# Scores one group ahead, and the mixer of one batch spread over the attention of the next

## The chip, the cores and the metric

The kernel runs on one core of a Trainium2 chip. The metric is the device time of one execution in microseconds (us). Not all kernels ran in the same rounds; before ran in all of them, and its median moved by 0.5 us between rounds. The profile is one further execution; its span is the time from the first to the last instruction, 1 to 4 us shorter than the timed runs.

## The reference, cut to what matters

Eight batches, each with a sequence of 3136 rows, 256 columns of u and v, 64 columns of z.

```python
def _attn_ref(u, v, z):                       # u, v: (8, 3136, 256); z: (8, 3136, 64)
    scores = np.matmul(z, z.transpose(0, 2, 1)) / S
    attn = np.maximum(scores, 0.0) ** 2
    return u * np.matmul(attn, v)

def _moe_ref(x, U, V, w_ch1, w_ch2):          # U: (3136, 32), V: (32, 3136), w: 256 to 1024 to 256
    h = x.transpose(0, 2, 1) @ U @ V
    u = x + h.transpose(0, 2, 1)
    ch = np.maximum(u @ w_ch1, 0.0) @ w_ch2
    return u + ch
```

The mixer of a batch needs `x.T @ U`, a sum over the whole sequence. It cannot begin before that batch's attention has ended. Different batches have nothing to do with each other.

## The kernel before

The sequence is padded to 25 tiles of 128 rows and handled in six groups of 512 columns and one narrow group of 128. For each group 13 pairs of score tiles are made (a pair fills one two-bank PSUM buffer, `ps2`, of which there are three), rectified, squared, and then multiplied with v into a one-bank buffer (`ps1`, two of them). "L169" in a profile line is line 169 of the kernel; the comments give these lines.

```python
for gi, (g0, gw) in enumerate(igroups):
    attn_sb = attn_pool.tile([P, NT, IGW], BF16, name="attn_sb")      # 2 buffers
    for jp in range(0, NT, 2):
        ps_s = ps2_pool.tile([P, 2, IGW], FP32, name="ps2")
        ...matmul(out=ps_s[:, jj, :gw], lhsT=zzT[...], rhs=zzT[:, g0 : g0 + gw])   # L169
        if (jp // 2) % 4 == 3:
            nc.vector.tensor_single_scalar(... op=ALU.max)            # L177, VectorE's share
        else:
            nc.scalar.activation(... func=AF.Relu)                    # L184, ScalarE's share
        nc.vector.tensor_tensor(... op=ALU.mult)                      # L189, the square
    for q0 in range(0, gtiles, 2):
        ...matmul(out=ps_o[:, qq, :], lhsT=attn_sb[...], rhs=v_bf[:, jt, :])       # L202
        ...x_bf = ps_o * u_sb                                         # L214, VectorE
# after the last group: t1 = U.T @ x (L223), copied on ScalarE (L231)
```

The mixer makes u2 transposed for all seven chunks first (L246 and L253, copied on ScalarE, L260). Then per chunk:

```python
for (c0, cw) in igroups:
    relu1_sb = relu1_pool.tile([P, NH, IGW], BF16, name="relu1_sb")   # 2 buffers
    for hp in range(0, NH, 2):
        ...16 matmuls in all, ps_m1 = w1.T @ u2T_bf                   # L270
        nc.scalar.activation(out=relu1_sb[...], in_=ps_m1, func=AF.Relu)           # L277
    for q0 in range(0, ctiles, 2):
        ...ps_f = t1 @ V + relu1 @ w2                                 # L289, L297
        ...out_sb = ps_f + x_bf, and the store                        # L305
```

The loop over the batches, with the weights loaded and cast ahead of it:

```python
emit_prep(0)          # z: load, cast, 25 transposes; v: 7 loads and casts (L150), all casts on ScalarE
for b in range(B):
    emit_attention(b)
    if b + 1 < B:
        emit_prep(b + 1)
    emit_mixer(b)
```

The order of these statements is not quite the order on an engine, since the framework that builds the kernel has a scheduler. In the trace of before, scores of the next group stand among the attention-times-v matmuls of this one, although the code has one block after the other.

## Time and profile before

| | before |
|---|---|
| time, median of 13 runs | 1374.5 us |
| span of the profile | 1372.8 us |
| TensorE matmuls laid end to end ("dense", worked out in the prediction) | 1262.7 us |
| start of the first batch's U matmuls | 134.6 us |
| steady period, from one batch's U to the next one's | 167.9 us |

The prediction shows the lines that carry its reading. One further line of the groups of before gives busy us and mean ns of one instruction, then the engine's idle time ahead of these instructions and what ended it:

```profile
L184 ACT ACTIVATE attn_sb<-ps 128x1024 bf16<-128x1024 f32 (+3 forms) x560 | 457.8, 912 | 390.1 <-PE ps L169 364.0
```

### The profile page before, as it was taken

How to read it: one execution, taken by the hardware profiler on the slowest of the kernel's cores; microseconds unless marked ns; L12 is line 12 of the kernel's file. 1: busy time of each engine (PE TensorE's matmuls, PEld its weight loads, DVE VectorE, ACT ScalarE, POOL GpSimd, SP SyncE). 2: the span in 40 equal slices, each digit the busy share in tenths (PEclk: the TensorE clock that was granted, in tenths of full speed). 3: DMA queues.
4: the chain of work that ended last, by engine and by line, in shares of the span. 5: the costliest groups of instructions: out<-in, count | busy, mean ns of one | idle time of the engine just before them, and what ended most of it. 6: DMA issues, size and time to landing. Idle time of an engine off the chain costs nothing.

```text
span 1372.8 us, 23038 instructions
## 1 busy us (share of the span) xinstructions
PE 1326.4 (97%) x10008; PEld 913.3 (67%) x10008; DVE 707.9 (52%) x1104; ACT 793.0 (58%) x976; POOL 23.7 (2%) x41
## 2 busy tenths in 40 slices
PE   3999999999999999999999999999999999999998
PEld 1677666676666766667666676666766667666665
DVE  1776147751477414774167732677217772177721
ACT  6854855557555575556655565655655555455554
POOL 2000000000000000000000000000000000000000
PEclk9999999999999999999999999999999999999999
DMA  9611421124111241111511115111131111111101
GB/s 236 183 32 31 145 70 32 32 64 134 49 32 32 65 148 41 32 32 57 148 49 32 32 49 159 38 32 32 57 102 33 32 32 34 62 34 32 32 32 65
DMA packets 109542, 87.89 MB, mean 64 GB/s; under 512 B 32832, under 2 KB 109120, under 8 KB 109440
## 3 DMA queue, kind: packets, MB, share of 16 engines
q1 hardware_dynamic: 109440, 86.41, 21.0%
q8 instruction: 78, 1.28, 0.4%
q14 instruction: 24, 0.20, 0.0%
HBM read 60.70 MB, written 25.69 MB: 63 GB/s over the span
## 4 chain that ended last, share of the span: by engine, by line
PE 75%; ACT 21%; DMA 2%; issue 1%; DVE 1%; ACTq 0%; SPq 0%; POOL 0%
PE ps L202 40%; PE ps L169 19%; ACT relu_sb L277 12%; PE ps L297 10%; ACT attn_sb L184 4%; PE ps L270 4%; ACT u2T_bf L260 3%; ACT zzT L135 2%; PE ps L223 2%; DMA v_raw<-in_v_dram 1%; PE ps L289 1%; ACT v_bf L150 0%; DMA wtmp<-in_moe_w_ch_dram 0%; DVE attn_sb L189 0%; DVE out_sb L305 0%
## 5 line engine op out<-in xcount | busy, mean ns | idle before, releaser
L184 ACT ACTIVATE attn_sb<-ps 128x1024 bf16<-128x1024 f32 (+3 forms) x560 | 457.8, 912 | 390.1 <-PE ps L169 364.0
L202 PE MATMUL ps<-v_bf,attn_sb 128*128 128x256 bf16 x5000 | 619.8, 273 | 1.2
L202 PEld LDWEIGHTS <-attn_sb 128*128 128x128 bf16 x5000 | 466.9, 98 | 164.3 <-DVE attn_sb L189 62.0
L189 DVE TENSOR_TENSOR attn_sb<-attn_sb 128x1024 bf16<-128x1024 bf16 (+3 forms) x728 | 407.0, 608 | 73.6 <-ACT attn_sb L184 71.3
L169 PE MATMUL ps<-zzT 128*128 128x512 bf16 (+1 forms) x1400 | 340.6, 357 | 9.8 <-ACT attn_sb L184 6.4
L305 DVE TENSOR_TENSOR out_sb<-ps,x_bf 128x512 f32<-128x512 f32 (+1 forms) x104 | 69.7, 671 | 405.6 <-PE ps L297 404.0
L277 ACT ACTIVATE relu_sb<-ps 128x1024 bf16<-128x1024 f32 (+1 forms) x224 | 190.9, 937 | 141.4 <-PE ps L270 141.4
L297 PE MATMUL ps<-w_bf,relu_sb 128*128 128x256 bf16 x1600 | 209.6, 273 | 7.9 <-ACT relu_sb L277 7.3
L169 PEld LDWEIGHTS <-zzT 128*128 128x128 bf16 x1400 | 133.4, 98 | 107.1 <-issue 29.3
L177 DVE TENSOR_SCALAR attn_sb<-ps 128x1024 bf16<-128x1024 f32 (+1 forms) x168 | 185.1, 1102 | 6.1 <-PE ps L169 6.1
L270 PE MATMUL ps<-u2T_bf,w_bf 128*128 128x512 bf16 (+1 forms) x896 | 183.9, 356 | 3.9 <-ACT u2T_bf L260 2.6
L297 PEld LDWEIGHTS <-relu_sb 128*128 128x128 bf16 x1600 | 148.6, 98 | 50.5 <-ACT relu_sb L277 24.5
L214 DVE TENSOR_TENSOR x_bf<-ps,u_sb 128x512 bf16<-128x512 f32 (+1 forms) x104 | 69.8, 671 | 176.8 <-PE ps L202 168.2
L270 PEld LDWEIGHTS <-w_bf 128*128 128x128 bf16 x896 | 83.2, 98 | 87.4 <-issue 7.9
L150 ACT CAST v_bf<-v_raw 128x1024 bf16<-128x1024 f32 (+1 forms) x56 | 52.0, 965 | 23.5 <-DMA v_raw<-in_v_dram 14.9
L289 PE MATMUL ps<-t_sb,V_bf 128*128 128x256 bf16 x200 | 53.4, 273 | 0.0
L260 ACT CAST u2T_bf<-ps 128x1024 bf16<-128x1024 f32 (+1 forms) x56 | 48.1, 995 | 0.9 <-PE ps L253 0.9
L246 PE MATMUL ps<-ident,x_bf 128*128 128x128 bf16 x400 | 41.8, 219 | 0.3
L128 PE MATMUL ps<-ident,z_bf 128*128 128x128 bf16 x200 | 20.9, 228 | 19.9 <-ACT z_bf L121 19.3
L253 PE MATMUL ps<-V_bf,t_sb 128*128 128x512 bf16 (+1 forms) x112 | 38.3, 356 | 0.0
L246 PEld LDWEIGHTS <-x_bf 128*128 128x128 bf16 x400 | 30.3, 97 | 10.7 <-issue 4.5
L128 PEld LDWEIGHTS <-z_bf 128*128 128x128 bf16 x200 | 16.2, 102 | 25.9 <-issue 22.1
(25 smaller groups left out, 151.8 us busy)
## 6 DMA issues: line engine op xcount, KB each, us to landing
v_raw<-in_v_dram SPq DMA_DIRECT2D x48, 512.0 KB, 4.7
u_sb<-in_u_dram SPq DMA_DIRECT2D x96, 256.0 KB, 2.7
out_dram<-out_sb SPq DMA_DIRECT2D x96, 256.0 KB, 2.1
z_raw<-in_z_dram SPq DMA_DIRECT2D x8, 768.0 KB, 5.3
wtmp<-in_moe_w_ch_dram SPq DMA_DIRECT2D x4, 512.0 KB, 4.1
v_raw<-in_v_dram SPq DMA_DIRECT2D x8, 64.0 KB, 2.2
u_sb<-in_u_dram SPq DMA_DIRECT2D x8, 64.0 KB, 2.1
out_dram<-out_sb SPq DMA_DIRECT2D x8, 64.0 KB, 2.0
```

The lines of the kernel that those rows point to most:

```text
L169: nc.tensor.matmul(out=ps_s[:, jj, :gw], lhsT=zzT[:, (jp + jj) * P : (jp + jj + 1) * P], rhs=zzT[:, g0 : g0 + gw], start=True, stop=True,)
L177: nc.vector.tensor_single_scalar(out=attn_sb[:, jp : jp + npair, :gw], in_=ps_s[:, :npair, :gw], scalar=0.0, op=ALU.max,)
L184: nc.scalar.activation(out=attn_sb[:, jp : jp + npair, :gw], in_=ps_s[:, :npair, :gw], func=AF.Relu,)
L189: nc.vector.tensor_tensor(out=attn_sb[:, jp : jp + npair, :gw], in0=attn_sb[:, jp : jp + npair, :gw], in1=attn_sb[:, jp : jp + npair, :gw] ...
L202: nc.tensor.matmul(out=ps_o[:, qq, :], lhsT=attn_sb[:, jt, q * P : (q + 1) * P], rhs=v_bf[:, jt, :], start=(jt == 0), stop=(jt == NT - 1),)
L214: nc.vector.tensor_tensor(out=x_bf[:, it0 : it0 + nq, :], in0=ps_o[:, :nq, :], in1=u_sb[:, :nq, :], op=ALU.mult,)
L246: nc.tensor.matmul(out=ps_u2[:, db, q * P : (q + 1) * P], lhsT=x_bf[:, it, db * P : (db + 1) * P], rhs=ident, start=(q == 0), stop=False,)
L260: nc.scalar.copy(out=u2T_bf[:, :, c0 : c0 + cw], in_=ps_u2[:, :, :cw])
L270: nc.tensor.matmul(out=ps_m1[:, hh, :cw], lhsT=w1_bf[:, db, ht * P : (ht + 1) * P], rhs=u2T_bf[:, db, c0 : c0 + cw], start=(db == 0), stop ...
L277: nc.scalar.activation(out=relu1_sb[:, hp : hp + 2, :cw], in_=ps_m1[:, :, :cw], func=AF.Relu,)
L297: nc.tensor.matmul(out=ps_f[:, qq, :], lhsT=relu1_sb[:, ht, q * P : (q + 1) * P], rhs=w2_bf[:, ht, :], start=False, stop=(ht == NH - 1),)
L305: nc.vector.tensor_tensor(out=out_sb[:, :nq, :], in0=ps_f[:, :nq, :], in1=x_bf[:, it0 : it0 + nq, :], op=ALU.add,)
```

## The change

The intent: TensorE should never wait for something made a moment ago. There are four parts. (1) Scores run one group ahead of the attention-times-v that reads them. (2) The mixer of batch b-1 is spread over the attention of batch b, chunk k beside group k, with its final matmuls one group later. (3) The next batch is prepared in group 4 and its first group is scored in the last group of this one, so that batches overlap. (4) The weights are loaded after the first batch's z and v. No matmul, relu or square is added or removed. The functions are cut into pieces that a new main loop calls in 13 slots per group; the core of the diff, with cuts marked:

```diff
-    u2t_pool = ctx.enter_context(tc.tile_pool(name="u2t", bufs=1))     # one tile for all chunks
+    u2t_pool = ctx.enter_context(tc.tile_pool(name="u2t", bufs=2))     # one tile per chunk
...
-    for dd in range(ND):        # weight loads and casts
+    def emit_weight_loads():
...
     emit_prep(0)
-    for b in range(B):
-        emit_attention(b)
-        if b + 1 < B:
-            emit_prep(b + 1)
-        emit_mixer(b)
+    emit_weight_loads()
+    emit_score_pairs(0, 0, 0, NPAIR)
+    finals = iter(())
+    for b in range(B):
+        m = b - 1
+        for k in range(NG):
+            if k == NG - 3 and b + 1 < B:
+                emit_prep(b + 1)
+            nxt = (b, k + 1) if k + 1 < NG else (b + 1, 0)
+            atv = attn_v_steps(b, k)
+            n_atv = igroups[k][1] // P * NT
+            done = 0
+            for slot in range(NPAIR):                       # 13 slots
+                if nxt[0] < B:
+                    emit_score_pairs(*nxt, slot, slot + 1)
+                upto = (slot + 1) * n_atv // NPAIR
+                advance(atv, upto - done)
+                done = upto
+                if slot in (0, 1, 3, 4):
+                    advance(finals, 1)
+                if m >= 0:
+                    if slot == 2:
+                        emit_u2T(m, k)
+                    if slot in (5, 7, 9, 11):
+                        emit_m1(m, k, (slot - 5) // 2, (slot - 5) // 2 + 1)
+            advance(atv, 1000)
+            advance(finals, 1000)
+            if m >= 0:
+                finals = final_steps(m, k)
+        emit_attention_tail(b)                              # U matmuls and t1
+    ...the mixer of the last batch, alone: u2T one chunk ahead, finals one chunk behind
```

In the changed kernel the lines are: L172 scores, L187 and L180 relus, L192 square, L247 attention-times-v, L278 U, L153 cast of v, L124 to L138 z, L302 to L316 u2T, L330 first layer, L337 its relu, L411 and L419 finals.

## The prediction

> **What bounds the kernel now.** I read the page first: the span, the busy shares, the chain by engine and line.
>
> ```profile
> span 1372.8 us, 23038 instructions
> PE 1326.4 (97%) x10008; PEld 913.3 (67%) x10008; DVE 707.9 (52%) x1104; ACT 793.0 (58%) x976; POOL 23.7 (2%) x41
> ...
> PE 75%; ACT 21%; DMA 2%; issue 1%; DVE 1%; ACTq 0%; SPq 0%; POOL 0%
> ```
>
> TensorE is the only full engine, and 75% of the chain that ends last is its matmuls. But 97% says little: a matmul's end is modelled and successive ones overlap, so short waits do not show as idle. I therefore looked in the chain in order of time for blocks where TensorE runs one kind of matmul without a break, to get its true pace:
>
> ```profile
> 56.02 1.08 PE ps L169 x5
> 57.10 6.12 PE ps L202 x56
> 63.22 1.08 PE ps L169 x5
> ...
> 73.97 6.12 PE ps L202 x56
> ...
> 161.19 3.45 PE ps L270 x16
> ```
>
> A matmul of 512 columns (L169, L270) takes 3.45/16 = 0.216 us, one of 256 columns (L202) 6.12/56 = 0.1093 us, and there is no price for changing kind (57.10 + 6.12 = 63.22). The 128-column ones come at 0.055 us (four in 0.22 us at 141.5 us of TensorE's timeline).
>
> One batch has 150 score, 96 first-MLP and 12 V matmuls of 512 columns (258), 625 attention-times-v, 25 U and 225 final ones of 256 (875), and 118 of 128 (scores and MLP of the last narrow group, transposes). That is 1251, times 8 is 10008, as the page counts. Dense they need 258 x 0.216 + 875 x 0.1092 + 118 x 0.0555 = 55.7 + 95.6 + 6.5 = 157.8 us a batch, 1262.7 us for eight. So 1372.8 - 1262.7 = 110 us are lost, and the next question is where. The windows of one steady attention group and one steady mixer chunk:
>
> ```profile
> 73.97:90.83 16.86, 16.83 (x127) 11.86 (x126) 12.56 (x18) 9.03 (x11) 0.00 (x0) 1.00 0.13 33
> ```
>
> ```profile
> 176.41:184.21 7.80, 7.60 (x55) 4.92 (x53) 1.38 (x2) 3.77 (x4) 0.00 (x0) 1.00 0.19 67
> ```
>
> The attention group has 25 scores and 100 of the 256-column ones: 5.40 + 10.92 = 16.3 us dense, 16.86 taken, 0.56 lost. The chunk has 16 x 0.216 + 36 x 0.1092 = 7.4 dense, 7.80 taken, 0.4 lost. VectorE is busy 12.56 of 16.86 in the one and 1.38 of 7.80 in the other: the two stages load the helpers very unequally. The timeline shows what a wait looks like:
>
> ```profile
> 66.81 0.60 PE L202 MATMUL ps<-v_bf,attn_sb 128*128 128x256 bf16 x4
> 67.30 0.59 PE L169 MATMUL ps<-zzT 128*128 128x512 bf16 x2
> 67.73 0.60 PE L202 MATMUL ps<-v_bf,attn_sb 128*128 128x256 bf16 x4
> 68.22 0.59 PE L169 MATMUL ps<-zzT 128*128 128x512 bf16 x2
> ...
> 180.78 0.38 PE L297 MATMUL ps<-w_bf,relu_sb 128*128 128x256 bf16 x2
> 181.36 0.39 PE L297 MATMUL ps<-w_bf,relu_sb 128*128 128x256 bf16 x2 [0.20 <-ACT relu_sb L277]
> ```
>
> In the attention, four matmuls of a pair that has only just been squared take 0.49 us instead of 0.44, pair after pair: TensorE goes at the pace of VectorE (four pairs cost VectorE 4 x 0.62 + 1.2 = 3.7 us, TensorE 4 x 0.915 = 3.66 us). In the mixer TensorE waits for ScalarE's relu of the same chunk. Both are waits for something made a moment ago, and the list of waits agrees:
>
> ```profile
> PEld L202 <- DVE attn_sb L189: 62.0, 259, 0.6
> ...
> PEld L297 <- ACT relu_sb L277: 24.5, 67, 0.5
> ```
>
> Last the start, where the large piece is:
>
> ```profile
> 12.32 0.57 SPq L77 DMA_DIRECT2D z_raw<-in_z_dram  x1
> ...
> 17.66 1.53 ACT L121 ACTIVATE z_bf<-z_raw 128x1600 bf16<-128x1600 f32 x1
> ...
> 19.33 1.01 PE L128 MATMUL ps<-ident,z_bf 128*128 128x128 bf16 x8 [19.33 <-ACT z_bf L121]
> ```
>
> The last rows of z are asked for only at 12.3 us, behind weights and v, so TensorE does nothing for 19.3 us.
>
> The U matmuls end a batch's attention; they start at 134.57 us in batch 0 and at 1311.7 in batch 7. Sorting the 110 us by these: up to 134.57 us 103.4 dense, so 31.2 lost (3.4 of it in six groups, 27.8 the start proper); then seven periods of (1311.72 - 134.57)/7 = 168.2 against 157.8, 10.3 lost each, 72 in all; the rest 61.1 against 54.4, 6.7 lost. A period's 10.3 is 6 x 0.56 = 3.4 in groups, 6 x 0.4 = 2.5 in chunks, and about 4.4 where batch and stage change.
>
> **What the Trainium skill says.** "TensorE: Matmul & The Clock Gate", section "Wait — 56ns, not 53.3ns?", gives the start-to-start time of warm matmuls as columns / 2.4 GHz plus about 2.5 ns: 215.7 ns for 512, and by the same formula (an estimate) 109.2 for 256. The trace agrees: 215.6 and 109.3, with a new weight load before each. "Perfetto Trace Analysis", section "Identifying the Most-Contended Engine", says matmul busy time is a bad measure of headroom; here 97% busy goes with 8% lost. The same page, section "Optimization Strategy", proposes to interleave regimes whose limiting engine differs, which is this change; the two windows show regimes that differ. Its section "Matmuls" wants independent groups to rotate through PSUM banks so that evacuation overlaps; the three two-bank buffers (ps2) and two one-bank buffers (ps1) stay as they are.
>
> **The change, part by part.** No matmul, relu or square is added or removed; the dense 1262.7 us stays. What moves is the order in which work is offered.
>
> 1. Scores run one whole group ahead of attention-times-v. A matmul then reads a square made some 16 us earlier, so the 0.05 us per alternation goes. VectorE needs 12.6 us per group of 16.3, ScalarE 9.0: as averages both fit. I leave 0.1 us per group. Saved per period: 3.4 - 0.6 = 2.8.
>
> 2. The mixer of batch b-1 is spread over the attention of batch b, chunk k beside group k, its final matmuls one group later still. The mixed group has 16.3 + 7.4 + 0.9 (u2T) = 24.6 us of TensorE, against 12.6 + 1.4 = 14 us of VectorE and 9.0 + 3.8 + 1.0 = 13.8 us of ScalarE. The 2.5 us of chunk waits nearly goes; I leave 0.5. The two-bank buffers now serve scores, u2T and MLP in turn. In a slot with both a score pair and an MLP pair TensorE has 0.43 + 0.84 + 0.86 = 2.1 us, ScalarE at most 2 x 0.93 = 1.9: it fits, narrowly.
>
> 3. Batch changes. The 4.4 us fall to about 2: the next batch's first group is already scored when this one's attention ends, and u2T no longer runs as a stage of its own that ScalarE paces (about 1 us of copy per chunk against 0.86 us of matmuls). What remains: in the narrow last group TensorE has about 13 us and ScalarE and VectorE about 11.5 each, and the next batch's preparation puts 1.5 + 7 x 0.55 + 6.5 = 12 us on ScalarE in one group (about 26 us beside TensorE's 26), which the light narrow scores of the following group must absorb. So a period loses 0.6 + 0.5 + 2 = about 3 instead of 10.3: 7 x 7.3 = 51 us saved.
>
> 4. Weights after z. z lands at about 1.2 + 5.3 = 6.5 us (the page's time from issue to landing), its cast takes 1.53: transposes at 8 us, 11 earlier. But before 19.3 us ScalarE had already done three weight and four v casts of 1.04 us, which now compete with the first relus; I give back 3 of the 11. The start loses 20 instead of 27.8, plus 0.6 for its groups.
>
> 5. The last mixer still runs alone, but a chunk's finals lie beside the next chunk's MLP: of 6.7 lost about 5 stay, 3.4 of them the closing output transfer.
>
> Sum: 1262.7 + 20.6 + 21 + 5 = 1309 us of span. The timed run is 1.7 us longer than the span (1374.47 against 1372.8), so **1310 us**, 4.7% less.
>
> **Rivals.** (a) VectorE stays the pacemaker: if the scheduler again puts squares just before their readers, part 1 saves nothing (7 x 2.8 = 20 us), about 1330. For it: VectorE is 75% busy in the attention. Against it: the dependence is now a group old.
> (b) The PSUM buffers become the wait that takes over: 42 full mixed chunks with four MLP pairs each, and a wait of 0.3 us at each is 50 us, about 1360. For it: 1.9 of 2.1 us in the tight slots. Against it: those slots alternate with plain ones, and VectorE takes every fourth score pair.
> (c) ScalarE overflows at preparation and batch change: 3 more us lost a period, 21 us, about 1331.
> (d) The start gains nothing because transfers (236 GB/s in the first slice of the page) and casts bound it: 8 us, 1318.
> (e) All goes well and a period loses only 1 us: about 1295.
>
> **Range and chances.** (e) and some of (a), (c), (d) together span 1292 to 1336. Staying above 1347 needs (b), or (a) and (c) at once. Faster by over 2%: 0.90; within 2%: 0.08; slower: 0.02. Slower would need head-of-line waits in the now longer interleaved TensorE order that none of the present rows shows.
>
> **What would show it.** Right: first transposes near 8 us; waits of weight loads for squares (62 us) and for the mixer's relu (24.5) mostly gone; a period near 161 us; a mixed group near 24.6 us; VectorE and ScalarE evenly busy over a period. Wrong: score or MLP matmuls that wait for a relu (a PSUM buffer), a gap at each batch change, ScalarE solid for tens of us at the start or at a preparation, or blocks of 256-column matmuls slower than 0.109 us when mixed, which would break the dense sum itself.

## More of the kernel before

The median of the runs is quoted; executions of one kernel lie within 0.25% of each other here.

The U matmuls close each batch's attention, so their starts cut the span into a start, seven periods and a rest, and each part can be held against its dense time.

A timeline of before in a steady group says how its idle time comes about (start, duration, engine, line, number of instructions; in brackets the idle time before and what ended it):

```profile
73.81 6.29 PE L202 MATMUL ps<-v_bf,attn_sb 128*128 128x256 bf16 x56
...
79.93 1.24 PE L169 MATMUL ps<-zzT 128*128 128x512 bf16 x5
...
80.34 7.10 ACT L184 ACTIVATE attn_sb<-ps 128x1024 bf16<-128x1024 f32 x8 [5.05 <-PE ps L169]
```

For 6 us TensorE does nothing but attention-times-v, and ScalarE has nothing to do for 5.05 us. Then the scores come, 20 of a group's 25 between 79.93 and 86.64 us, and ScalarE runs eight relus without a break: 7.10 / 8 = 0.89 us each.

VectorE has no break either, and for longer. A window from its first relu of that stretch to its last square (length, then busy us of TensorE, its weight loads, VectorE and ScalarE) shows it busy for all of 9.84 us:

```profile
80.77:90.61 9.84, 9.81 (x66) 5.98 (x64) 9.84 (x15) 7.06 (x9) 0.00 (x0) 1.00 0.12 28
```

The helpers' work is bunched: they idle in one stretch of a group and run solid in the other.

## The result, and the profile after

| | before | after |
|---|---|---|
| time, median | 1374.5 us | 1316.7 us |
| ratio, 95% interval | 1 | 0.9578 (0.9569 to 0.9588) |
| span | 1372.8 us | 1314.3 us |
| lost against dense | 110.1 us | 51.6 us |
| first U matmuls | 134.6 us | 135.2 us |
| steady period | 167.9 us | 161.7 us (161.4 to 162.0) |

A ratio is the mean time of one kernel's runs over that of before's runs in the same rounds, so it is not quite the ratio of the medians. The change is faster by 4.2%; 4.7% was predicted. The page of after, its first lines and its chain by engine:

```profile
span 1314.3 us, 23122 instructions
...
PE 1281.9 (98%) x10008; PEld 941.3 (72%) x10008; DVE 737.2 (56%) x1104; ACT 817.5 (62%) x976; POOL 23.7 (2%) x41
...
PE 87%; ACT 8%; DMA 4%; issue 1%; DVE 0%; POOL 0%; ACTq 0%; POOLq 0%
```

ScalarE's part of the chain fell from 21% to 8%. VectorE's busy tenths in 40 slices, first before and then after, show the stages mixed: the 1s and 2s of before are the mixers, in which VectorE had almost nothing to do.

```profile
DVE  1776147751477414774167732677217772177721
```

```profile
DVE  3886756555565556555565455664565546565411
```

The two big waits of the prediction, of weight loads for a square and for the mixer's relu, were 62.0 and 24.5 us. In the list of waits of after (us in total, times, longest) one is small and the other does not appear at all:

```profile
PEld L247 <- DVE attn_sb L192: 1.1, 3, 0.6
```

What TensorE's matmuls still wait for, in the same list:

```profile
PE ps L172 <- ACT attn_sb L187: 9.7, 15, 3.7
PE ps L131 <- ACT z_bf L124: 9.7, 1, 9.7
PE ps L172 <- ACT u2T_c L316: 5.6, 5, 1.7
```

One group without a mixer chunk (batch 0) and one with (batch 2), as windows (us of the window, then PE, PEld, VectorE, ScalarE, GpSimd busy, granted clock, share of the DMA engines, GB/s):

```profile
78.06:94.37 16.31, 16.31 (x127) 12.22 (x126) 13.15 (x19) 9.80 (x10) 0.00 (x0) 1.00 0.11 33
...
346.21:370.78 24.57, 24.57 (x189) 17.95 (x187) 14.70 (x20) 14.37 (x16) 0.00 (x0) 1.00 0.14 44
```

Both are dense: 16.3 and 24.6 us were worked out. A stretch of the mixed group shows the slots on TensorE; no row has a wait, and the first layer (L330), the scores (L172) and attention-times-v (L247) follow each other without a gap:

```profile
334.05 1.03 PE L330 MATMUL ps<-u2T_c,w_bf 128*128 128x512 bf16 x4
334.92 0.59 PE L172 MATMUL ps<-zzT 128*128 128x512 bf16 x2
335.35 0.93 PE L247 MATMUL ps<-v_bf,attn_sb 128*128 128x256 bf16 x7
...
337.42 1.03 PE L330 MATMUL ps<-u2T_c,w_bf 128*128 128x512 bf16 x4
```

(A duration here holds the modelled end of the last matmul; the pace is the difference of the starts.)

**Where the remaining 51.6 us are.** The first U matmuls start at 135.24 us and the last batch's at 1255.04.

- The start. Dense, TensorE has 103.4 us up to the first U, and now 1.4 us of transposes of batch 1 and 5.2 us of its scores besides: 110.0. Taken 135.2, so 25.2 lost (before: 31.2). Part of this is TensorE's granted clock: it fell towards the end of a wait of 3.73 us (to 19.13 us) and stayed at 0.50 until about 25 us. The ten scores and eight attention-times-v that start from 19.13 to 25.48 us took 6.35 us for 3.0 dense, 0.4 of it a wait, so about 3 us went to the clock (an estimate from these rows; for before, 0.77 over the 7.5 us from 26.80 gives 1.7).
- The seven periods take 1119.8 us against 1097.3 dense, so 22.5 lost. The five in the middle take 161.7 on average against 157.8, so 3.9 each. The last one, with no next batch to prepare, takes 151.6 against about 151.2. As the groups are dense, the loss belongs to the change of batches and the preparation.
- The rest takes 59.3 us against 55.4 dense, so 3.9 lost.

What a change of batch still loses can be read from the timeline around 308 us:

```profile
303.51 0.38 PE L309 MATMUL ps<-V_bf,t_sb 128*128 128x512 bf16 x1
...
303.90 1.03 ACT L187 ACTIVATE attn_sb<-ps 128x1024 bf16<-128x1024 f32 x1
...
306.17 1.04 ACT L153 CAST v_bf<-v_raw 128x1024 bf16<-128x1024 f32 x1 [1.25 <-DMA v_raw<-in_v_dram]
...
307.12 1.00 ACT L316 CAST u2T_c<-ps 128x1024 bf16<-128x1024 f32 x1
...
308.18 0.59 PE L172 MATMUL ps<-zzT 128*128 128x512 bf16 x2 [1.74 <-ACT u2T_c L316]
```

The u2T of a chunk was complete in PSUM just before 304 us, and ScalarE had no work from 304.93 on. But the next instruction in its queue was a cast of v whose transfer landed only at about 306.17. The u2T copy stood behind it, its PSUM buffer stayed occupied, and the scores that needed the buffer waited 1.74 us. The Trainium skill, "Perfetto Trace Analysis", section "Tensor Engine Instruction (MATMUL, LD_WEIGHTS)", calls the queues of ScalarE, VectorE and GpSimd strict FIFO. These rows agree: copyable work waited for 2.2 us (304.93 to 307.12), 1.25 of it for the cast's transfer and the rest for the cast itself. Two more places lose time in every period: the transposes with the u2T between 395.35 and 401.63 us take 6.28 us for 4.75 dense, and the narrow group of batch 2, up to 456.93 us, takes 13.46 for 12.94.

### The profile page after: what moved, and what is told of

It reads as the page before. It is cut to its first block, busy times and chain, and to the rows that moved or that the text cites.

```text
span 1314.3 us, 23122 instructions
## 1 busy us (share of the span) xinstructions
PE 1281.9 (98%) x10008; PEld 941.3 (72%) x10008; DVE 737.2 (56%) x1104; ACT 817.5 (62%) x976; POOL 23.7 (2%) x41
## 3 DMA queue, kind: packets, MB, share of 16 engines
q8 instruction: 78, 1.28, 0.4%
## 4 chain that ended last, share of the span: by engine, by line
PE 87%; ACT 8%; DMA 4%; issue 1%; DVE 0%; POOL 0%; ACTq 0%; POOLq 0%
PE ps L247 38%; PE ps L172 18%; PE ps L330 13%; PE ps L419 13%; ACT attn_sb L187 3%; DMA v_raw<-in_v_dram 3%; ACT zzT L138 2%; PE ps L411 2%; PE ps L302 1%; PE ps L309 1%; ACT v_bf L153 1%; DMA wtmp<-in_moe_w_ch_dram 1%; ACT relu_sb L337 1%; PE ps L278 1%; ACT u2T_c L316 0%
## 5 line engine op out<-in xcount | busy, mean ns | idle before, releaser
L247 PE MATMUL ps<-v_bf,attn_sb 128*128 128x256 bf16 x5000 | 659.9, 273 | 1.9 <-ACT zzT L138 1.6
L187 ACT ACTIVATE attn_sb<-ps 128x1024 bf16<-128x1024 f32 (+3 forms) x560 | 491.5, 896 | 234.6 <-PE ps L172 234.1
L192 DVE TENSOR_TENSOR attn_sb<-attn_sb 128x1024 bf16<-128x1024 bf16 (+3 forms) x728 | 432.4, 612 | 330.9 <-ACT attn_sb L187 328.2
L247 PEld LDWEIGHTS <-attn_sb 128*128 128x128 bf16 x5000 | 483.9, 98 | 177.4 <-issue 4.9
L172 PE MATMUL ps<-zzT 128*128 128x512 bf16 (+1 forms) x1400 | 388.7, 359 | 15.8 <-ACT attn_sb L187 9.7
L337 ACT ACTIVATE relu_sb<-ps 128x1024 bf16<-128x1024 f32 (+1 forms) x224 | 208.8, 933 | 196.6 <-PE ps L330 196.6
L180 DVE TENSOR_SCALAR attn_sb<-ps 128x1024 bf16<-128x1024 f32 (+1 forms) x168 | 186.1, 1108 | 94.5 <-PE ps L172 92.4
L330 PE MATMUL ps<-u2T_c,w_bf 128*128 128x512 bf16 (+1 forms) x896 | 209.2, 356 | 0.1
L419 PE MATMUL ps<-w_bf,relu_sb 128*128 128x256 bf16 x1600 | 207.3, 273 | 0.0
L172 PEld LDWEIGHTS <-zzT 128*128 128x128 bf16 x1400 | 136.2, 98 | 80.3 <-issue 23.8
L419 PEld LDWEIGHTS <-relu_sb 128*128 128x128 bf16 x1600 | 156.4, 98 | 21.9
L330 PEld LDWEIGHTS <-w_bf 128*128 128x128 bf16 x896 | 84.9, 98 | 52.9 <-issue 0.5
L316 ACT CAST u2T_c<-ps 128x1024 bf16<-128x1024 f32 (+1 forms) x56 | 51.8, 926 | 32.4 <-PE ps L309 32.4
L153 ACT CAST v_bf<-v_raw 128x1024 bf16<-128x1024 f32 (+1 forms) x56 | 53.9, 964 | 13.0 <-DMA v_raw<-in_v_dram 13.0
L411 PE MATMUL ps<-t_sb,V_bf 128*128 128x256 bf16 x200 | 54.5, 273 | 0.0
L302 PE MATMUL ps<-ident,x_bf 128*128 128x128 bf16 x400 | 41.6, 219 | 0.2 <-ACT attn_sb L187 0.2
L302 PEld LDWEIGHTS <-x_bf 128*128 128x128 bf16 x400 | 31.2, 98 | 8.6 <-issue 1.5
```

What stands on the lines that cost most here:

```text
L172: nc.tensor.matmul(out=ps_s[:, jj, :gw], lhsT=zzT[:, (jp + jj) * P : (jp + jj + 1) * P], rhs=zzT[:, g0 : g0 + gw], start=True, stop=True,)
L180: nc.vector.tensor_single_scalar(out=attn_sb[:, jp : jp + npair, :gw], in_=ps_s[:, :npair, :gw], scalar=0.0, op=ALU.max,)
L187: nc.scalar.activation(out=attn_sb[:, jp : jp + npair, :gw], in_=ps_s[:, :npair, :gw], func=AF.Relu,)
L192: nc.vector.tensor_tensor(out=attn_sb[:, jp : jp + npair, :gw], in0=attn_sb[:, jp : jp + npair, :gw], in1=attn_sb[:, jp : jp + npair, :gw] ...
L247: nc.tensor.matmul(out=ps_o[:, qq, :], lhsT=attn_sb[:, jt, q * P : (q + 1) * P], rhs=v_bf[:, jt, :], start=(jt == 0), stop=(jt == NT - 1),)
L302: nc.tensor.matmul(out=ps_u2[:, db, q * P : (q + 1) * P], lhsT=x_bf[:, it, db * P : (db + 1) * P], rhs=ident, start=(q == 0), stop=False,)
```

## The experiments

All kernels gave the right result; each was run four times in turn with before. "Ratio" is against before, with its 95% interval; us after a ratio is the median. Two pairs of theories were at stake. On the first gain: **age** says that TensorE lost time because it read things made a moment ago, so the lead of the scores and the later finals recover it by themselves; **load** says that the helpers are loaded unevenly between stages, so only mixing the stages helps. On what paces the attention: VectorE (the prediction's reading and its rival a), the PSUM buffers (rival b) or ScalarE (rival c).

### The weights after z, alone and taken back

b_weights_late is before with part 4 alone; a_weights_first is after without it.

```diff
 # b_weights_late (before)                   # a_weights_first (after)
-for dd in range(ND): ...weights             -emit_prep(0)
+def emit_weight_loads(): ...weights          emit_weight_loads()
 emit_prep(0)                                +emit_prep(0)
+emit_weight_loads()
```

> The kernel before with the weight loads offered after the first batch's preparation, nothing else. The sum of the prediction put this part at 8 us (transposes at 8 to 10 us instead of 19.3, some of it given back to casts on ScalarE): 1374 to about 1366. The rival, that ScalarE's casts and the transfers bound the start anyway, expects under 3 us.

> The changed kernel with the weights loaded ahead of z again, nothing else undone. If the late weights are worth the 8 us of the prediction the time rises from 1317 to about 1325; if the start is bound by casts and transfers, by under 3 us; in both cases over 85% of the gain stays, because it is made in the periods and not at the start.

Measured: b_weights_late 1367.8 us, 0.9953 (0.9938 to 0.9968), 6.7 us faster than before; a_weights_first 1321.9 us, 0.9618 (0.9602 to 0.9634), 5.2 us slower than after. So part 4 is worth 5 to 7 us, not the 8 that the prediction wrote down, and the rest of the change is worth about 52. In a_weights_first the first U comes at 142.96 us and its steady periods (161.1 to 161.7) are no longer than those of after, so the part acts on the start only.

### The mixer's finals one chunk later, alone

b_finals_late is before with the finals of a chunk emitted after the first layer of the next.

```diff
+        pending = None
         for (c0, cw) in igroups:
             ...first layer and relu of this chunk
-            ...finals of this chunk
+            if pending is not None:
+                emit_finals(b, *pending)
+            pending = (c0, cw, relu1_sb)
+        emit_finals(b, *pending)
```

> The kernel before with one thing done alone: in the mixer the final matmuls of a chunk are offered after the first-layer matmuls of the next chunk. Theory of age: the 0.4 us wait per chunk for the relu goes, a chunk falls from 7.80 to 7.4 us, 48 chunks give 17 to 20 us, 1374 to about 1356. Rival (ScalarE or the PSUM buffers pace the chunk whatever the order): under 5 us.

Measured: 1356.28 us, 0.9867 (0.9852 to 0.9881), 18.2 us faster than before. The starts of two chunks' first layers (L320 in this kernel) are 7.39 us apart, where before had 7.80 and the dense sum is 7.4:

```profile
163.76 3.62 PE L320 MATMUL ps<-u2T_bf,w_bf 128*128 128x512 bf16 x16
...
171.15 3.62 PE L320 MATMUL ps<-u2T_bf,w_bf 128*128 128x512 bf16 x16
```

The chunk becomes dense by age alone, with nothing mixed.

### The lead of the scores alone

b_lead_only has the slots with scores and attention-times-v only. The mixer is a stage of its own again, as before: all u2T, then each chunk with its finals at once; the weights come first. Since it is made from after, it also keeps the first half of part 3: the next batch is prepared in group 4 and its first group is scored in the last one.

```diff
     # from after
-    u2t bufs=2;  emit_prep(0);  emit_weight_loads()
+    u2t bufs=7;  emit_weight_loads();  emit_prep(0)
         ...in the slots:
-                if slot in (0, 1, 3, 4): advance(finals, 1)
-                ...emit_u2T and emit_m1 of batch b-1
         emit_attention_tail(b)
+        for k in range(NG): emit_u2T(b, k)
+        for k in range(NG): emit_m1(b, k, 0, 4); advance(final_steps(b, k), 1000)
```

> The kernel before with one thing done alone: scores offered one group ahead, in slots beside attention-times-v; weights first and the mixer as before. Prediction's part 1: 2.8 us a period, 22 us in all, about 1352. What the runs so far leave for it (ahead, finals late and weights late together gave 34.8, of which finals late 18.2 and weights late 6.7 alone): about 10, near 1364, because the saving inside the groups is partly given back at the stage change, where the late start of U and u2T is bare.

Measured: 1364.67 us, 0.9931 (0.9914 to 0.9947), 9.8 us faster than before. The groups become dense (16.39 us, from 16.86), which is worth 3 us a batch. But the steady period falls only from 167.9 to 167.2. The rest is given back where the stage changes:

```profile
145.79 0.27 PE L278 MATMUL ps<-x_bf,U_bf 128*128 128x256 bf16 x1 [0.89 <-DVE x_bf L261]
...
147.79 0.39 PE L302 MATMUL ps<-ident,x_bf 128*128 128x128 bf16 x4 [1.73 <-ACT t_sb L286]
```

With the scores done a group earlier, and the next batch's transposes already in group 4, TensorE has nothing left to put between the last attention-times-v and U, or between U and the u2T. It waits for x (0.89 us) and for t1 (1.73 us) with empty hands. Before had attention-times-v to run between its first U matmuls (299.9 to 302.6 us) and transposes of the next z right after them (from 305.09); this order has nothing. How much of the loss is the lead's and how much the early preparation's was not separated.

### All parts but the mixing

a_no_mix is after with its mixer run as a stage at the end of each batch, in the order that after itself uses for the last batch.

```diff
         ...in the slots:
-                if slot in (0, 1, 3, 4):
-                    advance(finals, 1)
-                if m >= 0:
-                    if slot == 2: emit_u2T(m, k)
-                    if slot in (5, 7, 9, 11): emit_m1(...)
         emit_attention_tail(b)
+        mixer_stage(b)      # after's own last loop: u2T one chunk ahead, finals one behind
```

> The changed kernel with scores one group ahead and finals one chunk later, but each mixer run as a stage of its own after its attention. Theory of age (a reader reads something made a group or chunk ago, mixing itself is not needed): groups stay at 16.3 to 16.4 us and chunks at 8.3 us with u2T, the only new loss is at the changes of stage, 1 to 3 us a batch: 1320 to 1340. Theory of evenness (the gain needs VectorE's and ScalarE's load spread over both stages): the 0.56 us per group and 0.4 per chunk come back, 40 us and more, 1355 or above.

Measured: 1339.64 us, 0.9746 (0.9731 to 0.976): 34.8 us faster than before, 22.9 slower than after. Groups are dense without any mixing, and the three single parts above sum up to nearly the same (6.7 + 18.2 + 9.8 = 34.7):

```profile
77.90:94.30 16.40, 16.40 (x127) 12.28 (x126) 13.24 (x19) 9.80 (x10) 0.00 (x0) 1.00 0.11 33
```

So for groups and chunks age is right, and load, as unevenness between stages, falls. Within a group age is not alone, though: the slots also spread the scores evenly, a pair every 1.3 us (13 in 16.40 us) instead of 20 scores in 6.7 us, and no run has the one without the other. What does mixing add then? Three lines of the list of waits of a_no_mix for TensorE:

```profile
PE ps L278 <- DVE x_bf L261: 10.1, 7, 1.4
...
PE ps L309 <- ACT t_sb L286: 8.9, 7, 1.5
PE ps L330 <- ACT u2T_c L316: 4.4, 6, 1.3
```

These three are a chain of dependences at the stage change, beside which nothing else is offered: x to U, U to t1 to u2T, u2T to the first layer. Together they are 10.1 + 8.9 + 4.4 = 23.4 us at the changes of stage, and none of them is among the waits of matmuls in after. The 22.9 us that mixing adds are near that, but not the same sum: after has 5.6 us of waits for u2T copies that a_no_mix has not. All waits of matmuls are 44.2 us in a_no_mix and 27.6 in after, so 16.6 less, where the spans differ by 21.8. The other 5 us go with the clock. At three of a_no_mix's changes of stage (near 141, 473 and 637 us) the granted clock fell to half for over 3 us, and at none of after's; for the first of them (the last three numbers are granted clock, DMA share, GB/s):

```profile
141.40:144.70 3.30, 2.93 (x15) 1.74 (x15) 0.00 (x0) 2.42 (x5) 0.00 (x0) 0.51 0.87 258
```

Each costs about 1.7 us of TensorE's work, by estimate from the clock over 5 us windows. The periods with such a fall are no longer than the others (164.7 to 165.1 against 164.6 to 164.8 us), since the wait for the u2T copy is then shorter: the chain sets the time. The use of mixing is that another batch's work lies beside this chain.

### VectorE's share of the relus, less and more

Three kernels move the share of relus that VectorE takes, from every fourth to every sixth or every second.

```diff
-                if (jp // 2) % 4 == 3:
+                if (jp // 2) % 6 == 5:        # b_dve6 (before): VectorE 2 of 13, ScalarE 11
+                if (jp // 2) % 2 == 1:        # b_dve2 (before), a_dve2 (after): VectorE 6 of 13
```

> The kernel before with VectorE taking every sixth score pair's relu instead of every fourth (2 of 13 instead of 3). If VectorE is what paces the alternation of scores and attention-times-v there (3.7 us for four pairs), it then needs 0.62 + 1.2/6 = 0.82 us a pair, ScalarE 0.78, both under TensorE's 0.87: the 0.05 us per pair goes, a group falls from 16.86 towards 16.4, up to 20 us in all, about 1355. If the wait is only the chain of latencies from score to square, the time stays within 5 us of 1374.

> The kernel before with VectorE taking every second score pair's relu (6 of 13). VectorE then needs 0.62 + 0.6 = 1.2 us a pair against 0.92 now; as pacemaker of some 7.5 alternating pairs a group it costs about 2.3 us a group, 48 groups: about 110 us, near 1480.

> The changed kernel with the same heavier VectorE share (6 of 13). A mixed group then has about 19 us of VectorE work in 24.6 us of TensorE work, and its squares are read a group later: no cost there. Only batch 0's six unmixed groups (about 17.5 us of VectorE in 16.3) and the batch changes slow: 10 to 20 us, 1327 to 1337. This is where mixing the stages, and not only age, should show; if age alone counted for nothing and VectorE paced each pair as before, it would cost 110 us here too.

Measured: b_dve6 1385.26 us, 1.008 (1.0065 to 1.0095); b_dve2 1392.33 us, 1.0132 (1.0117 to 1.0147); a_dve2 1309.59 us, 0.9529 (0.9515 to 0.9543), 7.1 us faster than after. All three forecasts missed. If VectorE alone had paced the attention of before, relieving it would have helped. It made before 11 us slower, because ScalarE then ran solid for longer:

```profile
81.36 8.85 ACT L184 ACTIVATE attn_sb<-ps 128x1024 bf16<-128x1024 f32 x10 [6.19 <-PE ps L169]
```

Ten relus in 8.85 us, after 6.19 us of nothing; the chain that ended last runs over the first four of them (3.78 us from 81.36 us). With more on VectorE (b_dve2) the chain does run over VectorE, as its rows show, but that costs 18 us and not 110:

```profile
81.06 0.88 PE ps L169 x4
81.96 1.22 DVE attn_sb L177
83.19 1.80 DVE attn_sb L189 x3
84.99 1.13 DVE attn_sb L177
86.12 1.20 DVE attn_sb L189 x2
```

So before sat between the two: both helpers run solid in the bunched part of a group, and moving a relu either way slows the whole. These runs can't say more, as each loads one helper with what it takes from the other; what relieving VectorE alone would do was not run. In the changed kernel, where the work is spread over a whole group, VectorE takes six relus of 13 and the kernel becomes faster, with ScalarE the one that is relieved: a_dve2 has its first U at 130.33 us instead of 135.24 (its clock stayed full up to there) and steady periods of 160.0 to 160.6 instead of 161.7.

### One two-bank PSUM buffer less

a_ps2_2 takes one of the three buffers that scores, u2T and first layer share.

```diff
-    ps2_pool = ...(name="ps2", bufs=3, ...);  ps1_pool = ...(name="ps1", bufs=2, ...)
+    ps2_pool = ...(name="ps2", bufs=2, ...);  ps1_pool = ...(name="ps1", bufs=4, ...)
```

> The changed kernel with two instead of three two-bank PSUM buffers for scores, u2T and first layer (the freed banks go to the one-bank pool). If those buffers are close to being the bound, as the rival (b) of the prediction held, each slot with two users now waits: 50 us or more. If their evacuation has the slack that the dense mixed groups suggest, under 15 us. My own view: a pair is evacuated about 1.3 us after its matmuls and the next use of its buffer comes one slot, 1.3 us, later, so it costs, 20 to 60 us.

Measured: 1327.29 us, 0.9658 (0.9642 to 0.9674), 10.6 us slower than after, with periods of 162.4 to 163.1 in the steady part. TensorE's list has scores waiting for a relu 12 times, 11.9 us in all, against 15 times and 9.7 us. With a third of these buffers gone (their banks went to `ps1`) a period grows by about 1 us; the PSUM buffers are not what bounds the changed kernel, and rival (b), sized at 50 us for three of them, falls. So does the view of 20 to 60 us.

### The casts of v on GpSimd

If ScalarE's queue is what waits at a change of batch and at the start, the seven casts of v per batch should leave it. GpSimd is idle 98% of after.

```diff
-            nc.scalar.copy(out=v_bf[:, c0 : c0 + cn, :], in_=v_raw[:, :cn, :])
+            nc.gpsimd.tensor_copy(out=v_bf[:, c0 : c0 + cn, :], in_=v_raw[:, :cn, :])
```

> The changed kernel with the casts of v on GpSimd instead of ScalarE. Theory: what a steady period still loses (161.4 to 162.0 us against 157.8 dense, while the last period, without a next batch, loses under 1) is ScalarE's queue at the batch change, where v casts that wait for their transfer stand ahead of u2T and of relus. Then a period falls by 1.5 to 2.5 us, in all 10 to 18 us: 1300 to 1307. Rival: the loss is the chain from the last scores to U and t1, or the transposes of z, and the casts do not matter: within 3 us of 1317; or GpSimd's casts slow VectorE and it gets slower.

Measured: 1304.38 us, 0.9491 (0.9477 to 0.9505), 12.3 us faster than after and the fastest kernel. The first U comes at 128.14 us (after 135.24), and the steady period is 160.1 (after 161.7). One wait of after is nearly gone:

```profile
PE ps L172 <- ACT attn_sb L187: 2.5, 8, 0.5
```

Scores waited 9.7 us for a relu in after, 2.5 here, and no matmul waits for a u2T copy any more. The cast in the groups, first of after and then of a_v_pool:

```profile
L153 ACT CAST v_bf<-v_raw 128x1024 bf16<-128x1024 f32 (+1 forms) x56 | 53.9, 964 | 13.0 <-DMA v_raw<-in_v_dram 13.0
```

```profile
L153 POOL CAST v_bf<-v_raw 128x1024 bf16<-128x1024 f32 (+1 forms) x56 | 64.5, 1159 | 180.8 <-PE ps L247 114.9 <-DMA v_raw<-in_v_dram 65.6
```

A cast is some 20% longer on GpSimd (spans there are rough) and the squares on VectorE 3% longer (630 ns against 612 on average), and the kernel is faster all the same. Of the 11.7 us by which the span is shorter, 7.1 come before the first U; the first period gives 3.3 back (163.0 after 159.7), and the five steady ones win 1.6 each. So ScalarE, rival (c), is behind a good part of what after still loses at the start and at a change of batch, though not all of it: 160.1 is still 2.3 above the dense 157.8.

Two things limit this reading. Whether it is the place of the casts in the queue that counts, or only the amount of ScalarE's work, is not separated: a_dve2 has the same steady period (160.1 on average) with the casts still on ScalarE, where they waited for transfers as long as in after (13.4 us against 13.0). And of the 7.1 us before the first U an estimated 3 are the clock, which was 0.59 in after from 17.20 to 24.70 us and stayed full here:

```profile
17.20:24.70 7.50, 7.12 (x44) 4.03 (x44) 7.50 (x11) 7.15 (x9) 3.50 (x5) 1.00 1.19 289
```

Here it fell later, to 0.68 over the 5 us from 135 us, which is 1.6 us by estimate of the 3.3 that the first period gives back.

### The start by itself, and all together

a_start removes what the trace shows ahead of the first transposes: a one-element ScalarE instruction first, so that the 1.28 us table load need not wait for z; z of batch 0 in two parts; and the casts of the weights on GpSimd. a_all3 is a_start, the casts of v on GpSimd, and every third relu on VectorE.

```diff
+    nc.scalar.copy(out=warm2, in_=warm)                       # one element per partition
-            nc.scalar.copy(out=w1_bf[...], in_=wtmp)          # and w2, U, V likewise
+            nc.gpsimd.tensor_copy(out=w1_bf[...], in_=wtmp)
+        zcuts = [0, 4, NT] if b == 0 else [0, NT]             # z: load and cast per part
 # a_all3 besides:
-            nc.scalar.copy(out=v_bf[...], in_=v_raw[...])
+            nc.gpsimd.tensor_copy(out=v_bf[...], in_=v_raw[...])
-            if (jp // 2) % 4 == 3:
+            if (jp // 2) % 3 == 2:
```

> The changed kernel with three things at the start only: a one-element ScalarE copy first, so that the table load (1.28 us, now after z has landed) is out of the way, the first four row tiles of z loaded and cast apart, and the weights cast on GpSimd. Before the first U matmuls the changed kernel loses 25 us against the dense sum where the prediction had 20.6. Theory: ScalarE's casts and the late first transposes are this loss: 6 to 12 us less, 1305 to 1311. Rival: transfers of v bound the start: under 3 us.

> Start as in the run before, v casts on GpSimd, and VectorE taking every third score pair's relu: the candidate for the best version. If the parts add: 1317 - 8 - 14 - some 2 = about 1293; if they share the same ScalarE relief, about 1300.

Measured: a_start 1312.95 us, 0.9553 (0.9539 to 0.9567), 3.7 us faster than after; a_all3 1317.02 us, 0.9583 (0.9568 to 0.9597), no faster than after and 12.6 slower than a_v_pool. In a_start the first transposes begin at 3.69 us, 6 us earlier than in after, but the first U at 132.75, only 2.5 us earlier:

```profile
3.69 0.59 PE L138 MATMUL ps<-ident,z_bf 128*128 128x128 bf16 x4 [3.69 <-ACT z_bf L131]
...
7.98 0.61 PE L138 MATMUL ps<-ident,z_bf 128*128 128x128 bf16 x4 [3.70 <-ACT z_bf L131]
...
19.37 0.59 PE L179 MATMUL ps<-zzT 128*128 128x512 bf16 x2 [2.81 <-ACT attn_sb L194]
```

The head start is spent waiting, for the second part of z and then for relus behind casts of v. Up to the first U, then, the casts of v cost more (7.1 us in a_v_pool) than the table load, the undivided z and the weight casts together (2.5). In both the clock has a share: from 20 to 25 us it was 0.50 in after and 0.66 in a_start. The 3.7 us fall between the 6 to 12 of the theory and the rival's under 3.

a_all3 was expected at 1293 to 1300. It has the earliest first U of all, at 127.99 us, but its steady periods are 161.8 us (two) and 163.4 (three), where a_v_pool has 160.1. Its list shows a wait that after does not have, and a_v_pool only once, for 1.1 us:

```profile
PE ps L285 <- DVE x_bf L268: 11.2, 6, 2.1
```

The U matmuls wait six times for x, which VectorE makes, five of them for 2.06 us. That is about what 161.8 has over 160.1. The step from 161.8 to 163.4 goes with the clock: right after three of these five equal waits, those that end at 618.84, 782.27 and 945.70 us, it fell to half, and these are the three longer periods:

```profile
619.40:622.60 3.20, 3.20 (x16) 2.11 (x14) 0.69 (x1) 1.14 (x2) 0.89 (x1) 0.50 0.78 252
```

VectorE has more relus here, and its squares are slower (644 ns on average). Two things differ from a_v_pool in the steady part, the weights being loaded once only: the share of the relus (every third, where a_dve2 had every second), and through it the order that the scheduler chose. Which of them makes U wait was not separated and stays open. It does say that gains of single edits (7 us of a_dve2, 12 of a_v_pool) need not add up. The start of a_start with the casts of a_v_pool alone was not run.

## Why the prediction was right

The time was 1316.7 us against 1310, inside the range of 1292 to 1336. It was right in direction and, by and large, in mechanism; the terms of its sum were off one by one, and their errors partly cancel. By its steps:

- **The dense sum** held. A plain group takes 16.31 us (16.3 worked out), a mixed one 24.57 (24.6), and no matmul became slower by being mixed.
- **Where the 110 us of before lie.** The split was right in kind, with one slip: its end mark, 1311.72 us, is where the last 23 of the U matmuls begin; two single ones lie before it, the first at 1308.93. So the period of before is 167.8 us and not 168.2, and the rest loses 9.5, not 6.7.
- **"TensorE goes at the pace of VectorE"** is the step that failed. VectorE does run solid in that stretch, but it is not alone: less work on it made before slower by 11 us where 20 faster was expected, more made it slower by 18 and not 110. The work is bunched: both helpers run solid in one part of a group, and ScalarE idles for 5 us in the other. The mistake was to conclude a pacemaker from 3.7 us against 3.66 on one engine. The same sum for ScalarE, 3 x 0.89 = 2.7 us, would have given it room; only the timeline shows it solid. It did no harm to the time, since the cure (scores a group ahead) is the same for both.
- **Part 1** was to leave 0.6 us a period in the groups, **part 2** 0.5: nothing is left of either. But part 1 alone gives 9.8 us and not the 20 of seven times 2.8, because the stage change takes the rest back; that comes only with the mixing.
- **Part 3**, the change of batches, was sized at 2 us a period and is 3.9 in the steady periods. The prediction had counted the preparation's 12 us on ScalarE but as load, beside 26 us of TensorE. What the rows show is order: a cast that waits for its transfer at the head of the queue (1.74 us). That the load has no part in it is not shown, as a_dve2 says. By accident the terms of parts 1 to 3 balance: 3.1 predicted and 3.2 measured over the seven periods, 21 us and 22.5.
- **Part 4**, the start, was sized at 20.6 us lost and is 25.2. The first transposes come at 9.71 us and not at 8: the table load starts only when z has landed, at 6.73 us. More comes from the casts of v on ScalarE, for which the prediction gave back 3 us together with the weights: without them the first U comes 7.1 us earlier, 3.3 of which the next period takes back. The prediction also took TensorE at full clock after the first transposes, and after the wait shown here about 3 us were lost to a halved one. In the rows of that start two casts of v, at 15.60 and 17.11 us, fall in the cut just ahead of the relu at 18.06 us, for which the scores wait 3.73 us:

```profile
6.73 1.28 ACT L124 ACT_TABLE_LOAD   x1 [6.73 <-DMA z_raw<-in_z_dram]
8.03 1.54 ACT L124 ACTIVATE z_bf<-z_raw 128x1600 bf16<-128x1600 f32 x1
...
9.71 1.01 PE L131 MATMUL ps<-ident,z_bf 128*128 128x128 bf16 x8 [9.71 <-ACT z_bf L124]
...
18.06 1.02 ACT L187 ACTIVATE attn_sb<-ps 128x1024 bf16<-128x1024 f32 x1
...
19.13 1.01 PE L172 MATMUL ps<-zzT 128*128 128x512 bf16 x2 [3.73 <-ACT attn_sb L187]
```

- **Part 5**, the rest: 5 us predicted, 3.9 measured. (The dense time there is 55.4 us, 1.0 more than without the change, as the narrow chunk's finals of batch 6 now fall into it.)
- **The sum**: 20.6 + 21 + 5 = 46.6 us were to stay lost, 25.2 + 22.5 + 3.9 = 51.6 are. These 5.0 us, 0.7 us more between span and timed run (2.4 instead of 1.7) and the rounding make the difference of 6.7.
- **The rivals.** (a) and (b) did not happen: waits for squares fell to 1.1 us, and a buffer less costs 10.6 us, not 50. (c) did, at a smaller size than its 21 us: the batch change loses 1.9 us more than assumed in each of five periods, and a_v_pool recovers 1.6 of them. (d) happened in part: the weights' move is worth 5 to 7 us where (d) said nothing and the sum said 8. Of the signs of being wrong that the prediction named, one came, in small: scores waited 9.7 us for a relu and 5.6 for a u2T copy, at the start, at preparations and at changes of batch.

## What to carry to other kernels

Interleaving two stages pays where a chain of dependences leaves the bounding engine with nothing to do; within the stages it was enough here to make each thing one step before it is read, which needs no mixing. Read a group's timeline, not only its averages: an engine that is 60% busy may be full in one half of a group and idle in the other. Look at the granted clock beside every wait of TensorE: here waits of 1 to 4 us were followed, in some cases and not in others, by 3 us or more at half clock. And once the bounding engine is dense, look for instructions that wait for a transfer at the head of a helper's queue, and try them on an idle engine, even if it is slower at them.

## What the Trainium skill lacked or had wrong

- "TensorE: Matmul & The Clock Gate", section "Back-to-back issue gap": it gives 131 ns at 512 columns and 81 ns at 128 for a sustained stream of weight load and matmul, and calls its other formula one for isolated matmuls only. The streams, with a new weight load each, run at 215.6 ns (3.45 us for 16) and 55 ns (0.22 us for 4), which is what the "isolated" formula gives, and what the section cited in the prediction says of back-to-back matmuls.
- The same page, section "What's actually happening", has the clock released after one window of about 3.4 us of sustained activity and throttled after an idle one, and does not say what a partly busy window counts. The clock fell to half after waits shorter than that window: in a_all3 after three of five waits of 2.06 us each, and not after the other two. In after, TensorE is busy for 5.17 us of this stretch of the start, 7.5 us long, and has a mean clock of 0.59 in it:

```profile
17.20:24.70 7.50, 5.17 (x16) 2.22 (x16) 4.47 (x6) 7.02 (x8) 0.00 (x0) 0.59 1.11 293
```

- "Perfetto Trace Analysis", section "Optimization Strategy", advises to interleave regimes with different limiting engines, besides optimizing within each, but does not say where the gain is to be sought. Here the regimes became dense without interleaving (34.8 us), and the interleaving gave 22.9 us more by filling the changes of stage, whose chain of dependences had 23.4 us of waits in the list.
- The same page, section "Optimizing GPSIMD Operations", prefers other engines wherever possible. Here moving the casts of v to GpSimd (1159 ns against 964) gained 12.3 us, as it took 53.9 us of casts and 13.0 us of waits for their transfers off ScalarE. Which of the two counted is open.
